# Layer B's gate in the reciprocal's argument at a memory read, and eleven token-row buffers in place of ten

## The chip, the cores and the metric

The kernel runs on one core of a Trainium2 chip. The metric is device time in microseconds (us), as the median of several runs. The kernel before took 1744.88, 1745.94 and 1742.05 us in three runs: median 1744.88 us.

A core has a matrix engine, TensorE (PE; its weight loads are shown apart as PEld), and VectorE (DVE), ScalarE (ACT) and GpSimd (POOL) for the rest. SyncE (SP) does nothing here but issue transfers; ACT and POOL issue some as well. An engine executes its instructions in the order in which they were written to it, so an instruction that waits holds all behind it. Matrix products come to rest in PSUM, of which the kernel uses eight banks of 128 partitions x 512 float32. Everything else lies in SBUF, in buffers that a pool gives out: a new tile takes over the place of an older one, and its first writer waits until the older tile's last reader is done.

## The reference

Four layers A, B, A, B, each added to its input, which is normalised first; 2048 tokens of 640 features, 32 heads of 20 features.

```python
def _A_ref(x, wqkv, wo):                       # linear attention
    phi = lambda t: jnp.where(t > 0, t + 1, jnp.exp(t)) + 1e-6
    pq, pk = phi(q), phi(k)
    kv = jnp.einsum("bhsd,bhse->bhde", pk, v)
    z = jnp.einsum("bhsd->bhd", pk)
    num = jnp.einsum("bhqd,bhde->bhqe", pq, kv)
    den = jnp.einsum("bhqd,bhd->bhq", pq, z)[..., None] + 1e-6
    o = num / den
    return (...)(o, 0, 2, 1, 3).reshape(B, S, D) @ wo

def _B_ref(x, wq, wk, wv, wo, beta):           # attention in 4 segments of 512, with a memory
    g = _sigmoid(beta).reshape(1, H, 1, 1)
    for s in range(N):
        qs, ks, vs = q[:, :, s], k[:, :, s], v[:, :, s]
        p = _softmax(jnp.einsum("bhqd,bhkd->bhqk", qs, ks) * scale + mask, axis=-1)
        a_dot = jnp.einsum("bhqk,bhkd->bhqd", p, vs)
        pq = phi(qs)
        num = jnp.einsum("bhld,bhde->bhle", pq, M)
        den = jnp.einsum("bhld,bhd->bhl", pq, z)[..., None] + 1e-6
        a_mem = num / den
        o = g * a_mem + (1.0 - g) * a_dot
        outs.append(o)
        pk = phi(ks)
        M = M + jnp.einsum("bhld,bhle->bhde", pk, vs)
        z = z + jnp.einsum("bhld->bhd", pk)
    return (...)(jnp.stack(outs, 2)...).reshape(B, S, D) @ wo

x = x + _A_ref(_layernorm(x), A_wqkv, A_wo)
x = x + _B_ref(_layernorm(x), B_wq, B_wk, B_wv, B_wo, B_beta)
...                                            # and both once more
```

The gate g has one value per head: it weighs what is read from the memory against what comes from the segment's own attention.

## The kernel before, in words

**Tiling.** The tokens go in four segments of 512, each of four tiles of 128 tokens (`NT`). A tile of tokens is a *row*: 128 partitions (tokens) x 640 features, 2,560 bytes per partition. For a projection a row is transposed on PE (`turn`, L325), and ACT copies the result from PSUM as fp16 (L329) while DVE writes the remainder, also as fp16 (L330); a projection is then three fp16 products per 128 features, 15 matmuls of 128x320 for half a row (`proj_n`, L401) or 15 of 128x512 for 128 features of a segment (`proj_t`, L387).

**Two streams.** One generator writes the projections and everything that goes with them (`dense`), another the attention of layer B (`attention`): per group of four heads the two fp16 parts of queries and keys are loaded (`stacks`, L994), PE makes scores (L1008) from which DVE takes row maxima (L1015); the maxima are transposed, copied by ACT (L1035) and written into the query stack by two short transfers on SP's queue (L1038); PE makes the scores again with keys on the partitions (L1050), ACT takes exponentials (L1054, tile `pe`), POOL clears what lies over the diagonal (`affine_select`, L1061), PE sums with the values (L1077), ACT evacuates (L1083), and after a transposition the group's 80 features are added to the segment's output `otok` (L1097, L1101). The two streams are woven by modelled costs, and the result is the order on PE, which is kept as written (`MANUAL = ("PE",)`). On the other engines and on the transfer queues a scheduler sets the order: it goes through the program with modelled times, gives each instruction a place when its inputs and its buffer would be free, and so a different number of buffers can give a different order there.

**Row buffers.** Ten buffers of 2,560 bytes per partition are shared by all rows, of whatever kind:

```python
ROWS = 10
return self.sb.tile([P, C, 2, P], F16, tag="row", name="oT", bufs=ROWS)
```

The kinds that occur below: `xo`, the input that is added to a layer's output (loaded, L336); `xn`, a row of that sum; `oT`, a row of attention output, transposed; `x` and `xh`, a loaded row and its normalised form; `pk`, keys of layer A.

**Segment 2's output beside layer 3's first pass.** When the second layer's last segments are still attended to, segment 2's output projection and the first pass of the third layer over segment 0 (`g_first`, with its memory() products, L566) run woven with it, at about 780 to 907 us:

```python
yield from weave(self.g_first(0, x[0], wA, L, over(segs[2])),
                 chain(loads(1), when(segs[2], "attended", out[2]), norms(1)))
```

`out[2]` is `b_out`. Per row it takes an `xo` and an `xn` from the row buffers, starts on the transposition of the next row into another `oT`, and makes the two halves of `xn` in `o_half`: ACT copies a half from PSUM (L478), POOL adds `xo` (L479). The store of `xn` stands on ACT's queue (L977). DVE then gathers the row's moments for the next normalisation, in which `g_norms` takes an `xh` per row, transposes it, and converts it on ACT to fp16 (L514), the remainder on POOL (L515).

```python
x = self.load_x(src, s, i, "xo")
xn = self.row("xn")
t = turned(i + 1) if i + 1 < NT else iter(())
for n in range(2):
    yield from (c for c in [next(t, None)] if c)
    self.o_half(oT[i], wo, "B", x, xn, n, later=not st.get("ends"))
```

**The memory.** `b_project` sums phi(k) v and phi(k) per head as blocks of 128 features (`acc`), with columns of 21 per head: 20 for the numerator, one for the denominator. Blocks off the diagonal are cleared by a product with a pattern, `masked` (L758); the pattern for a read is `gblk` (128x756 float32, 3,024 bytes per partition), which has g in the numerator's columns and 1 in the denominator's. `gates` makes it at the start of the program: g = 1 / (1 + exp(-beta)) by ACT and DVE (L211 is the reciprocal), a copy of the plain pattern `blk` (L214) and five products (L218). `read_mem` reads a memory for one tile of tokens in two halves of 16 heads: matmuls (L456), denominator + 1e-6 (L463), reciprocal (L464), product (L465). Layer A reads its memory by the same function with the plain pattern.

Of the kernel before, what the change touches and what calls it, by code (L numbers as in the profile page):

```python
# [9 lines left out]
F32 = mybir.dt.float32  # L10
F16 = mybir.dt.float16
BF16 = mybir.dt.bfloat16
I32 = mybir.dt.int32
AF = mybir.ActivationFunctionType
OP = mybir.AluOpType
# [5 lines left out]
S, D, H, DH = 2048, 640, 32, 20  # L21
P = 128
C = D // P
SEG = 512
# [3 lines left out]
E1 = DH + 1  # L28
# [6 lines left out]
LO = [(P * t) // DH for t in range(C)]  # L35
HI = [(P * t + P - 1) // DH for t in range(C)]
WID = [(HI[t] - LO[t] + 1) * E1 for t in range(C)]
OFF = [sum(WID[:t]) for t in range(C)]
MW = sum(WID)
VW = H * E1 + 11  # L40
HB = H // 2
# [86 lines left out]
def pause(n):  # L128
    for _ in range(n):
        yield 0.0  # L130
# [12 lines left out]
class Kernel:  # L143
# [14 lines left out]
    def row(self, name):  # L158
        return self.sb.tile([P, D], F32, tag="row", name=name, bufs=ROWS)

# [35 lines left out]
    def gates(self):  # L196


        nc, cp = self.nc, self.cp
        beta = self.A["B_beta"]  # L200
        g = cp.tile([P, H], F32, name="gate")
        nc.sync.dma_start(g, bass.AP(tensor=beta.tensor, offset=beta.offset, ap=[[0, P], [1, H]]))
        self.cg = cp.tile([P, NG], F32, name="cg")
        nc.vector.memset(self.cg, -1e4)
        for h4 in range(4):
            nc.sync.dma_start(self.cg[32 * h4 + DH:32 * h4 + DH + 1],
                              bass.AP(tensor=beta.tensor, offset=beta.offset + h4, ap=[[0, 1], [4, NG]]))
        nc.scalar.activation(g, g, AF.Exp, scale=-1.0)
        nc.scalar.activation(self.cg, self.cg, AF.Exp)
        nc.vector.tensor_scalar(g, g, 1.0, None, op0=OP.add)  # L210
        nc.vector.reciprocal(g, g)  # L211
        nc.vector.tensor_scalar(self.cg, self.cg, 1.0, 2.0 ** 100, op0=OP.add, op1=OP.min)
        self.gblk = cp.tile([P, MW], F32, name="gblk")
        nc.vector.tensor_copy(self.gblk, self.blk)  # L214
        for t in range(C):
            n = HI[t] - LO[t] + 1
            b = self.gblk[:, OFF[t]:OFF[t] + WID[t]].rearrange("p (h e) -> p h e", e=E1)[:, :, :DH]
            nc.vector.tensor_tensor(b, b, g[:, LO[t]:HI[t] + 1, None].to_broadcast([P, n, DH]), op=OP.mult)  # L218

    def w_src(self, key):  # L220
        L, n = key
# [220 lines left out]
        self.vu[k] = user  # L442
        return self.vt[k]

    def read_mem(self, pq, mem, dst):

        nc, sb = self.nc, self.sb
        cut = HB * E1
        for k in range(2):
            nd = self.bank()  # L450
            cost, first = 0, True
            for t in range(C):
                a, b = LO[t] * E1, LO[t] * E1 + WID[t]
                lo, hi = max(a, k * cut), min(b, (k + 1) * cut)
                if lo < hi:
                    nc.tensor.matmul(nd[:, lo - k * cut:hi - k * cut], pq[t],  # L456
                                     mem[:, OFF[t] + lo - a:OFF[t] + hi - a],
                                     start=first, stop=True, skip_group_check=True)
                    first = False
                    cost += 4 * (hi - lo) * COL  # L460
            nd = nd[:, :cut].rearrange("p (h e) -> p h e", e=E1)
            rc = sb.tile([P, HB], F32, tag="rc", name="rc", bufs=3)
            nc.vector.tensor_scalar(rc, nd[:, :, DH], 1e-6, None, op0=OP.add)  # L463
            nc.vector.reciprocal(rc, rc)  # L464
            nc.vector.tensor_tensor(dst[:, k * HN:(k + 1) * HN].rearrange("p (h e) -> p h e", e=DH),  # L465
                                    nd[:, :, :DH], rc[:, :, None].to_broadcast([P, HB, DH]),
                                    op=OP.mult)
            yield cost

    def new_oT(self):  # L470
        return self.sb.tile([P, C, 2, P], F16, tag="row", name="oT", bufs=ROWS)

# [51 lines left out]
    def g_first(self, s, box, w, L, behind=None):  # L524
# [7 lines left out]
        def keys(i):  # L532
            pk.append(sb.tile([P, 2, D + 1], F16, tag="row", name="pk", bufs=ROWS))
            nc.gpsimd.memset(pk[i][:, 0, HN:HN + 1], 1.0)
# [55 lines left out]
    def merge(self, L, wv, wo, memory, fill):  # L590
# [45 lines left out]
        for t in range(C):  # L636
# [3 lines left out]
            for n in range(2):  # L640
                a, b = max(lo, n * HN), min(hi, (n + 1) * HN)
                for c in range(C if a < b else 0):
                    for k, m in ((0, 0), (0, 1), (1, 0)):
# [3 lines left out]
                        first = False  # L647
            k2 = sb.tile([P, 2, SEG], F16, tag="row", name="kt", bufs=ROWS)
            nc.vector.memset(k2, 0.0)
# [217 lines left out]
    def b_project(self, st):  # L867

        nc, sb, bp = self.nc, self.sb, self.bp
        s, w, xT, acc = st["s"], st["w"], st["xT"], st["acc"]  # L870
# [11 lines left out]
        def pk_turn():  # L882
            pt = self.bank()
            for i in range(NT):
                nc.tensor.transpose(pt[:, i * P:(i + 1) * P], pkT[:, i * P:(i + 1) * P], self.ident)
            pk = bp.tile([P, SEG], F32, tag="pkt", name="pkt", bufs=1)
            nc.scalar.activation(pk, pt, AF.Copy)
            return pk
# [13 lines left out]
        for t in range(C):  # L902
            p = yield from self.proj_t(xT, w["q"], t)
            self.split_store(p, st["qd"], t, "q")
            if s > 0:
                pq = sb.tile([P, SEG], F32, tag="pq", name="pq", bufs=PQ)
# [7 lines left out]
            p = yield from self.proj_t(xT, w["k"], t)  # L914
# [10 lines left out]
        def rest():  # L925
            if s == 0:
                yield from pause(4)
            if s < NSEG - 1:
                pk = pk_turn()
                yield 440  # L930
                update(C - 1, pk)
                yield 4 * 4 * WID[C - 1] * COL
                st["mem"] = self.masked(acc, self.gblk)
        st["rest"] = rest()

    def b_memory(self, st, mem):
        st["o"] = self.sb.tile([P, NT, D], F32, tag="big", name="otok", bufs=3)
        if st["s"] > 0:
            for i in range(NT):
                yield from self.read_mem([q[:, i * P:(i + 1) * P] for q in st["pq"]], mem, st["o"][:, i])  # L940
        st["remembered"] = True

    def b_spill(self, st):
# [55 lines left out]
    def row_max(self, G, todo):  # L999

        nc, bp, qs, ks = self.nc, self.bp, G["qs"], G["ks"]
        bs = [self.bank() for _ in range(2)]
        cost = 0
        for p, i, a in todo:
            n = (i + 1) * P
            for par in range(2):
                r = slice(64 * par, 64 * par + 60)
                nc.tensor.matmul(bs[par][:, a:a + n], qs[r, p, i * P:(i + 1) * P], ks[r, p, :n],  # L1008
                                 start=True, stop=True)
                cost += n * COL  # L1010
        for par in range(2):
            for p, i, a in todo:
                n = (i + 1) * P
                junk = bp.tile([P, SEG], BF16, tag="junk", name="junk", bufs=1)
                nc.vector.tensor_tensor_reduce(bs[par][:, a:a + n], bs[par][:, a:a + n], self.maskw[:, SEG - n:],  # L1015
                                               1.0, NEG, OP.add, OP.max, G["mg"][:, par, p, i:i + 1])
        return cost
# [307 lines left out]
                        a.cost = max(a.cost, d.cost)  # L1325


ROWS = 10
PQ = 5
QUEUES = ('gpsimd', 'scalar', 'sync', 'sync', 'gpsimd', 'sync')  # L1330
PE_BUFS = 10
# [33 lines left out]
```

## Time and profile before

| | |
|---|---|
| median of three runs | 1744.88 us |
| the profiled execution | 1743.11 us |
| its span, first to last instruction | 1741.4 us |
| granted clock of TensorE (mean) | 0.998 |
| busy: PE, PEld | 1668.7 us, 1048.4 us |
| busy: DVE, ACT, POOL | 1183.8, 969.3, 518.7 us |
| time on the chain that ended last | PE 77%, DVE 10%, ACT 6% |

PE's time without work is 1741.4 - 1668.7 = 72.7 us. By stretches of the span, worked out from the busy time of each:

| stretch, us | PE idle, us | what runs |
|---|---|---|
| 0 to 100 | 15.0 | start, weights, layer 1 |
| 100 to 200 | 2.7 | layer 1 |
| 200 to 780 | 15.3 | layers 1 and 2 |
| 780 to 840 | 2.0 | attention of layer 2, first pass of layer 3 |
| 840 to 907 | 6.9 | the same, with segment 2's output |
| 907 to 1080 | 0.9 | end of layer 2, layer 3 |
| 1080 to 1741 | 29.5 | layers 3 and 4 |

How lines of the profile are read: a group of instructions stands as line, engine, operation, written tile <- read tiles, partitions x elements, count, then busy time and mean duration in ns of one, then the idle time of the engine before them and what ended most of it. In a timeline a row stands as start, duration, engine, line, operation and tiles, and in square brackets how long the engine had stood idle before and which instruction's end released it. SPq and ACTq are the parts of SP and ACT that issue transfers, and a row that begins "DMA" is a transfer from issue to landing.

### The profile page before, as it was taken

Reading aid. Unit: us, or ns where it says so; the run is one execution under the profiler, and the core shown is the slowest. Engines: PE = TensorE matmul, PEld = TensorE weight load, DVE = VectorE, ACT = ScalarE, POOL = GpSimd, SP = SyncE. Lnnn points to the kernel's source line nnn. Section 1 sums busy time; section 2 is a strip of 40 time slices with the busy share of each in tenths; the row PEclk is TensorE's granted clock in tenths of the full one; section 3 lists DMA queues with packets and bytes.
Section 4 is the critical chain, followed back from the end, with each engine's and each line's share of the span. In section 5 each row is a group of like instructions: output and inputs, shape, how many; then the busy total and the mean of one; then the engine's idle time right before and its main releaser. Section 6 shows DMA issues by size and latency. Waiting matters only on the chain.

```text
span 1741.4 us, 36031 instructions
## 1 busy us (share of the span) xinstructions
PE 1668.7 (96%) x13032; PEld 1048.4 (60%) x13032; DVE 1183.8 (68%) x3856; ACT 969.3 (56%) x1818; POOL 518.7 (30%) x982
## 2 busy tenths in 40 slices
PE   6999999999999999999989999999999999999998
PEld 4676666654665566456556777666546545645555
DVE  8645534577787677758864466846778877878773
ACT  5545433357557646667665553333675576666674
POOL 1543350022123312333342311220422432333452
PEclk9999999999999999999999999999999999999999
DMA  7422453422322322352211303433232323223432
GB/s 264 181 109 95 155 188 105 136 70 81 118 69 70 113 93 81 124 191 67 78 43 39 114 31 122 159 105 124 66 105 83 112 80 106 102 81 111 137 108 92
DMA packets 118330, 187.59 MB, mean 108 GB/s; under 512 B 13948, under 2 KB 79612, under 8 KB 115848
## 3 DMA queue, kind: packets, MB, share of 16 engines
q1 hardware_dynamic: 105896, 142.68, 25.7%
q0 software_dynamic: 3040, 21.63, 3.4%
q10 hardware_dynamic: 9216, 20.98, 3.1%
q8 instruction: 103, 1.69, 0.4%
q14 instruction: 75, 0.61, 0.1%
HBM read 106.05 MB, written 78.64 MB: 106 GB/s over the span
## 4 chain that ended last, share of the span: by engine, by line
PE 77%; DVE 10%; ACT 6%; issue 2%; POOL 2%; DMA 2%; SPq 0%; ACTq 0%; POOLq 0%; DVEq 0%
PE ps L401 32%; PE ps L387 17%; PE ps L1077 8%; PE ps L1050 4%; PE ps L1008 3%; ACT pe L1054 3%; PE ps L325 3%; PE ps L566 3%; PE ps L456 3%; DVE ps L1015 2%; PE ps L1090 1%; PE ps L893 1%; PE ps L732 1%; DVE st L344 1%; DVE oT L330 1%
## 5 line engine op out<-in xcount | busy, mean ns | idle before, releaser
L1015 DVE CUSTOM_DVE_ANT_0 ps<-ps,maskw 128x512 f32<-128x512 f32 (+3 forms) x1024 | 472.8, 520 | 40.4 <-PE ps L1008 38.1
L1054 ACT ACTIVATE pe<-ps,lsc 128x512 f32<-128x512 f32 x640 | 395.0, 696 | 91.1 <-PE ps L1050 88.0
L1061 POOL TENSOR_SCALAR_AFFINE_SELECT pe<-pe 128x256 f32<-128x256 f32 (+1 forms) x640 | 230.1, 365 | 448.8 <-ACT pe L1054 434.9
L401 PEld LDWEIGHTS <-xT 128*128 128x128 f16 x2880 | 280.6, 98 | 114.8 <-issue 10.2
L401 PEld LDWEIGHTS <-oT 128*128 128x128 f16 x1920 | 186.1, 98 | 80.3 <-issue 6.5
L1077 PE MATMUL ps<-pe,v 128*32 128x512 f32 (+3 forms) x2048 | 161.4, 436 | 13.3 <-POOL pe L1061 6.9
L401 PE MATMUL ps<-w_Bo,oT 128*128 128x320 f16 x960 | 142.4, 301 | 2.5 <-ACT pe L1054 1.0
L1015 DVE DVE_READ_ACCUMULATOR2_ANT mg<- 128x1 f32 x1024 | 144.7, 141 | 0.0
L387 PE MATMUL ps<-xT,w_Bq 128*128 128x512 f16 x600 | 140.2, 379 | 1.9 <-ACT pe L1054 0.8
L401 PE MATMUL ps<-w_Bv,xT 128*128 128x320 f16 x960 | 139.7, 299 | 0.7 <-DVE otok L1097 0.6
L387 PE MATMUL ps<-xT,w_Bk 128*128 128x512 f16 x600 | 138.8, 379 | 1.2 <-ACT pe L1054 1.2
L401 PE MATMUL ps<-w_Ak,xT 128*128 128x320 f16 x960 | 136.1, 299 | 0.5 <-ACT r L415 0.5
L1008 PE MATMUL ps<-ks,qs 60*128 60x512 f16 (+3 forms) x1024 | 124.6, 297 | 8.9 <-ACT pe L1054 3.2
L858 DVE SCALAR_TENSOR_TENSOR nat<-ps,nat 128x512 f16<-128x512 f32 x80 | 55.2, 690 | 87.9 <-ACT nat L857 87.8
L1077 PEld LDWEIGHTS ps<-pe,v 128*32 128x32 f32 x2048 | 64.9, 109 | 73.4 <-issue 44.9
L1050 PE MATMUL ps<-qs,ks 62*128 62x512 f16 (+3 forms) x1024 | 105.7, 300 | 3.1 <-ACT pe L1054 1.1
L427 POOL TENSOR_SCALAR e<-e 128x320 f32<-128x320 f32 (+1 forms) x52 | 82.9, 1595 | 82.1 <-ACT e L423 77.9
L857 ACT ACTIVATE nat<-ps 128x512 f16<-128x512 f32 x80 | 48.2, 603 | 90.9 <-PE ps L387 71.6
L387 PEld LDWEIGHTS <-w_Bk 128*128 128x128 f16 x600 | 57.3, 98 | 65.4 <-issue 5.6
L387 PEld LDWEIGHTS <-w_Bq 128*128 128x128 f16 x600 | 56.7, 98 | 65.8 <-issue 7.8
L1008 PEld LDWEIGHTS <-qs 60*128 60x128 f16 x1024 | 50.3, 94 | 75.0 <-issue 47.7
L349 POOL TENSOR_TENSOR rs<-rs,mhalf 128x1 f32<-128x1 f32 x48 | 27.6, 576 | 218.7 <-DVE rs L348 218.7
(220 smaller groups left out, 2633.1 us busy)
## 6 DMA issues: line engine op xcount, KB each, us to landing
x<-xn ACTq DMA_DIRECT2D x48, 320.0 KB
qs<-qd SPq DMA_DIRECT2D x128, 120.0 KB
ks<-kd SPq DMA_DIRECT2D x128, 120.0 KB
xo<-x SPq DMA_DIRECT2D x48, 320.0 KB
pqi<-pqd SPq DMA_DIRECT2D x32, 320.0 KB
qd<-nat SPq DMA_DIRECT2D x40, 256.0 KB
kd<-nat SPq DMA_DIRECT2D x40, 256.0 KB
x<-in_A_x SPq DMA_DIRECT2D x16, 320.0 KB
```

What stands on the lines that cost most here:

```text
L325: nc.tensor.transpose(pt[:, (c - c0) * P:(c - c0 + 1) * P], src[:, c * P:(c + 1) * P], self.ident)
L387: nc.tensor.matmul(p, w[:, c, a, t * P:(t + 1) * P], xT[:, c, b, :], start=k == 0, stop=k == 3 * C - 1)
L401: nc.tensor.matmul(p, xT[:, c, a, i * P:(i + 1) * P], w[:, c, b, n * HN:(n + 1) * HN], start=k == 0, stop=k == 3 * C - 1)
L427: nc.gpsimd.tensor_scalar(e, e, 1.0, eps, op0=OP.min, op1=OP.add)
L456: nc.tensor.matmul(nd[:, lo - k * cut:hi - k * cut], pq[t], mem[:, OFF[t] + lo - a:OFF[t] + hi - a], start=first, stop=True, skip_group_ch ...
L858: nc.vector.scalar_tensor_tensor(nat[:, 1], p, QK_SHIFT, nat[:, 0], op0=OP.mult, op1=OP.subtract)
L1008: nc.tensor.matmul(bs[par][:, a:a + n], qs[r, p, i * P:(i + 1) * P], ks[r, p, :n], start=True, stop=True)
L1015: nc.vector.tensor_tensor_reduce(bs[par][:, a:a + n], bs[par][:, a:a + n], self.maskw[:, SEG - n:], 1.0, NEG, OP.add, OP.max, G["mg"][:, p ...
L1050: nc.tensor.matmul(b[:, a:a + n], ks[r, p, j * P:(j + 1) * P], qs[r, p, j * P:], start=True, stop=True)
L1054: nc.scalar.activation(e, b, AF.Exp, scale=self.lsc)
L1061: nc.gpsimd.affine_select(d, d, pattern=pat, compare_op=OP.is_ge, fill=0.0, base=0, channel_multiplier=-1)
L1077: nc.tensor.matmul(G["pv"][32 * h4:32 * h4 + 32, j * P:], v[j][:, h * E1:h * E1 + 32], G.pop((p, par, j)), start=j == 0, stop=j == 2, skip ...
```

## The change

`gates` stops at 1 + exp(-beta), which `self.ginv` keeps; the reciprocal, the tile `gblk`, its copy and its five products are gone. A layer B memory is now masked with the plain pattern. In `read_mem`, layer B passes `ginv`, and the argument of the reciprocal is made in one instruction with two tensor operands, (denominator + 1e-6) * (1 + exp(-beta)); its reciprocal is g / (denominator + 1e-6). Layer A passes nothing and keeps its form. In `row_max` a tile `junk` (128x512 bf16, 1,024 bytes per partition), which nothing reads or writes, is no longer asked for. The rows go from ten buffers to eleven.

```diff
@@ gates
         nc.vector.tensor_scalar(g, g, 1.0, None, op0=OP.add)
-        nc.vector.reciprocal(g, g)
         nc.vector.tensor_scalar(self.cg, self.cg, 1.0, 2.0 ** 100, op0=OP.add, op1=OP.min)
-        self.gblk = cp.tile([P, MW], F32, name="gblk")
-        nc.vector.tensor_copy(self.gblk, self.blk)
-        for t in range(C):
-            n = HI[t] - LO[t] + 1
-            b = self.gblk[:, OFF[t]:OFF[t] + WID[t]].rearrange("p (h e) -> p h e", e=E1)[:, :, :DH]
-            nc.vector.tensor_tensor(b, b, g[:, LO[t]:HI[t] + 1, None].to_broadcast([P, n, DH]), op=OP.mult)
+        self.ginv = g
@@ read_mem
-    def read_mem(self, pq, mem, dst):
+    def read_mem(self, pq, mem, dst, ginv=None):
...
-            nc.vector.tensor_scalar(rc, nd[:, :, DH], 1e-6, None, op0=OP.add)
+            if ginv is None:
+                nc.vector.tensor_scalar(rc, nd[:, :, DH], 1e-6, None, op0=OP.add)
+            else:
+                nc.vector.scalar_tensor_tensor(rc, nd[:, :, DH], 1e-6, ginv[:, k * HB:(k + 1) * HB],
+                                               op0=OP.add, op1=OP.mult)
             nc.vector.reciprocal(rc, rc)
@@ b_project, rest()
-                st["mem"] = self.masked(acc, self.gblk)
+                st["mem"] = self.masked(acc, self.blk)
@@ b_memory
-                yield from self.read_mem([q[:, i * P:(i + 1) * P] for q in st["pq"]], mem, st["o"][:, i])
+                yield from self.read_mem([q[:, i * P:(i + 1) * P] for q in st["pq"]], mem, st["o"][:, i],
+                                         self.ginv)
@@ row_max
-                junk = bp.tile([P, SEG], BF16, tag="junk", name="junk", bufs=1)
@@
-ROWS = 10
+ROWS = 11
```

PE's order is the same in both programs. On DVE, ACT, POOL and SP rows move in the stretch described above, where segment 2's output runs beside layer 3's first pass. The line numbers of the changed program are smaller by up to eight: its L476, L477 and L976 are L478, L479 and L977 of before, its L323 is L329, L330 is L336, L361 is L367, L1033, L1036, L1052, L1059, L1081 and L1099 are L1035, L1038, L1054, L1061, L1083 and L1101.

ACT before, at the row of segment 2's output whose `xn` is written first in the stretch. `pe` are exponentials, `oT` copies the next transposed row (3 and then 2 of its 5 blocks), `mt` the maxima, `oTf` the evacuated sums, `xn` the two halves of the output row, and DMA its store:

```order
L1054 ACTIVATE pe<-ps,lsc 128x512 x4
L329 ACTIVATE oT<-ps 128x3x128
L329 ACTIVATE oT<-ps 128x2x128
L1054 ACTIVATE pe<-ps,lsc 128x512 x2
L1035 ACTIVATE mt<-pm 32x128
L1083 ACTIVATE oTf<-ps,cg 128x512
L1054 ACTIVATE pe<-ps,lsc 128x512 x4
L478 ACTIVATE xn<-ps,ioB 128x320 x2
L1054 ACTIVATE pe<-ps,lsc 128x512
L977 DMA x_88<-xn 128x640
L1054 ACTIVATE pe<-ps,lsc 128x512 x4
L478 ACTIVATE xn<-ps,ioB 128x320 x2
```

The same place after:

```order
L323 ACTIVATE oT<-ps 128x2x128
L407 ACTIVATE e<-ps,inv_Aq 128x320
L409 ACTIVATE r<-ps,inv_Aq 128x320
L1052 ACTIVATE pe<-ps,lsc 128x512 x4
L476 ACTIVATE xn<-ps,ioB 128x320 x2
L1052 ACTIVATE pe<-ps,lsc 128x512 x2
L976 DMA x_88<-xn 128x640
L1033 ACTIVATE mt<-pm 32x128
L1081 ACTIVATE oTf<-ps,cg 128x512
L476 ACTIVATE xn<-ps,ioB 128x320
L1052 ACTIVATE pe<-ps,lsc 128x512 x4
L476 ACTIVATE xn<-ps,ioB 128x320
```

The copies of `oT` have moved ahead of the exponentials of the group before and of layer 3's queries (L407, L409); both halves of the first `xn` and its store stand one batch of exponentials earlier; and the halves of the second `xn` come one at a time, on either side of the next four exponentials.

POOL before, at the same place. `pe` are the selects on the exponentials, `xn` the additions of `xo`, `otok` the addition of a group of heads, `rs` the power in the moments of a segment:

```order
L1101 TENSOR_TENSOR otok<-otok,tmp 128x4x80
L1061 AFFINE_SELECT pe<-pe 128x128 x4
L479 TENSOR_TENSOR xn<-xn,xo 128x320 x2
L1061 AFFINE_SELECT pe<-pe 128x2x128 x5
L479 TENSOR_TENSOR xn<-xn,xo 128x320 x2
L1061 AFFINE_SELECT pe<-pe 128x2x128
L367 TENSOR_TENSOR rs_12196<-rs_12196,mhalf 128x4
```

POOL after:

```order
L1059 AFFINE_SELECT pe<-pe 128x2x128 x4
L477 TENSOR_TENSOR xn<-xn,xo 128x320 x2
L1059 AFFINE_SELECT pe<-pe 128x2x128 x2
L477 TENSOR_TENSOR xn<-xn,xo 128x320
L1099 TENSOR_TENSOR otok<-otok,tmp 128x4x80
L1059 AFFINE_SELECT pe<-pe 128x128 x4
L477 TENSOR_TENSOR xn<-xn,xo 128x320
L1059 AFFINE_SELECT pe<-pe 128x2x128 x4
L361 TENSOR_TENSOR rs_11684<-rs_11684,mhalf 128x4
```

The first `xn`'s additions have moved ahead of the last two wide selects of the group before and of the four narrow ones after them; the second `xn`'s stand around those four.

SP before, in the same stretch. `qs<-mt` writes maxima into a query stack, `qs<-qd` and `ks<-kd` load the stacks, `pqd` stores layer 3's queries:

```order
L552 DMA pqd_0_10215<-e 128x320 x2
L1038 DMA qs<-mt 2x8x128 x2
L994 DMA qs<-qd 60x2x512 x2
L994 DMA ks_2759<-kd 60x2x512 x2
L336 DMA xo<-x_87 128x640
L1038 DMA qs<-mt 2x8x128 x4
```

SP after:

```order
L550 DMA pqd_0_9823<-e 128x320 x2
L330 DMA xo<-x_87 128x640
L1036 DMA qs<-mt 2x8x128 x2
L993 DMA qs<-qd 60x2x512 x2
L993 DMA ks_2751<-kd 60x2x512 x2
L1036 DMA qs<-mt 2x8x128 x4
```

The load of `xo` has moved ahead of two writes of maxima and of the loads of a group's stacks.

## The prediction

> **What bounds the kernel now.** I read the page's busy shares and chain first, then the busy time by stretches, to find where TensorE (PE) is not working, then the timelines of the engines in the one stretch where the row buffers are waited for.
>
> ```profile
> PE 1668.7 (96%) x13032; PEld 1048.4 (60%) x13032; DVE 1183.8 (68%) x3856; ACT 969.3 (56%) x1818; POOL 518.7 (30%) x982
> ...
> PE 77%; DVE 10%; ACT 6%; issue 2%; POOL 2%; DMA 2%; SPq 0%; ACTq 0%; POOLq 0%; DVEq 0%
> ```
>
> PE bounds the kernel: it is busy for 1668.7 of 1741.4 us. The order on PE is written out by the kernel and the change leaves it alone, so time can come only out of the 72.7 us in which PE stands idle, and go only into new idle time. So: which of those idle places does a row buffer make?
>
> ```profile
> 40.00:60.00 20.00, 18.23 (x133) 12.99 (x131) 15.84 (x36) 14.46 (x29) 10.10 (x7) 1.00 0.37 130
> 60.00:80.00 20.00, 20.00 (x111) 11.98 (x110) 12.28 (x37) 8.46 (x12) 11.83 (x11) 1.00 0.72 251
> ...
> 780.00:840.00 60.00, 57.98 (x525) 36.99 (x518) 53.58 (x198) 43.63 (x89) 24.23 (x51) 1.00 0.29 94
> 840.00:907.00 67.00, 60.13 (x514) 35.20 (x512) 47.51 (x172) 40.72 (x77) 25.34 (x52) 1.00 0.19 58
> 907.00:1080.00 173.00, 172.12 (x1314) 123.49 (x1313) 91.39 (x210) 95.34 (x195) 34.53 (x67) 1.00 0.21 70
> ```
>
> Columns: stretch, length, busy time of PE, PEld, DVE, ACT, POOL. From 780 to 840 us PE idles 60.00 - 57.98 = 2.02 us, 3.4%. From 840 to 907 us, where the same attention runs beside segment 2's output and the third layer's first pass, it idles 67.00 - 60.13 = 6.87 us, 10%, though DVE, ACT and POOL are all less busy per us there. From 907 to 1080 us it idles 0.88 us in 173. Whatever is won before 907 us is therefore carried on: what follows is PE's own work in a fixed order.
>
> ```profile
> 856.27 0.55 PE L325 MATMUL ps<-ident,otok 128*128 128x128 f32 x3
> ...
> 863.63 2.21 PE L401 MATMUL ps<-w_Bo,oT 128*128 128x320 f16 x15
> ...
> 874.13 2.20 PE L401 MATMUL ps<-w_Bo,oT 128*128 128x320 f16 x15 [0.20 <-ACT pe L1054]
> ...
> 877.50 0.63 PE L1008 MATMUL ps<-ks,qs 60*128 60x384 f16 x4 [0.63 <-DVE oT L330]
> ...
> 900.12 0.63 PE L1077 MATMUL ps<-pe,v 128*32 128x256 f32 x6 [1.81 <-POOL pe L1061]
> ```
>
> ```profile
> 876.37 0.76 ACT L329 ACTIVATE oT<-ps 128x384 f16<-128x384 f32 x2 [1.13 <-PE ps L401]
> ...
> 890.62 0.94 ACT L478 ACTIVATE xn<-ps,ioB 128x320 f32<-128x320 f32 x2 [2.77 <-PE ps L401]
> ...
> 892.94 0.36 ACTq L977 DMA_DIRECT2D x<-xn  x1
> 893.34 2.46 ACT L1054 ACTIVATE pe<-ps,lsc 128x512 f32<-128x512 f32 x4 [1.20 <-POOL pe L1061]
> 897.43 0.94 ACT L478 ACTIVATE xn<-ps,ioB 128x320 f32<-128x320 f32 x2 [1.63 <-DMA x<-xn]
> ```
>
> Read these together. The three transposes of 856.27 wait in a PSUM bank until 876.37, when ACT copies them out; what ends that copy's wait is not the transpose but the projection that ended at 876.33 (874.13 + 2.20), the last reader of the older oT whose row the new oT takes. The two projections of 863.63 and 874.13 fill one xn; ACT takes both halves at 890.62, when the next projection has read its oT. That is 16 to 25 us of bank time for results that were finished. The next xn (897.43) waits for a store of an earlier xn, and everything queued behind it on ACT and POOL waits too: PE then stands 1.81 us. So in this stretch the wait that ends last is often for one of ten row buffers, and PE feels it as a full bank or a late exponential.
>
> **The change part by part.**
>
> *Start.* Seven DVE instructions go.
>
> ```profile
> L211 DVE RECIPROCAL gate<-gate x1: 333/333/333, 41.2 to 41.2; 128x32 f32<-128x32 f32 x1
> ...
> L214 DVE CAST gblk<-blk x1: 545/545/545, 74.6 to 74.6; 128x756 f32<-128x756 bf16 x1
> ...
> L218 DVE TENSOR_TENSOR gblk<-gblk,gate x5: 296/298/319, 75.7 to 76.6; 128x140 f32<-128x140 f32 x4, 128x160 f32<-128x160 f32 x1
> ```
>
> They cost 0.33 + 0.55 + 5 x 0.30 = 2.4 us of DVE. At 74.6 to 76.9 us PE is busy for all of its slice (20.00 of 20.00): nothing gained. At 41.2 us PE's slice has idle time, so that one is worth 0 to 0.33 us; I take 0, since PE's work of that slice waits on weights and not on the gate.
>
> *Masks.* Six products of a memory read the plain pattern in place of the gated one.
>
> ```profile
> L758 DVE TENSOR_TENSOR mem<-acc,gblk x6: 932/946/948, 347.9 to 1490.2; 128x756 f32<-128x756 f32 x6
> L758 DVE TENSOR_TENSOR mem<-acc,blk x1: 945/945/945, 242.8 to 242.8; 128x756 f32<-128x756 f32 x1
> ```
>
> The plain pattern already stands in one row: 945 against 946 ns. Cost 0.
>
> *Gate at the read.* Layer B's memory reads, 48 by the first row below, take a scalar_tensor_tensor with a second tensor operand where a tensor_scalar stood.
>
> ```profile
> L465 DVE TENSOR_TENSOR otok<-ps,rc 128x320 f32<-128x320 f32 x48 | 23.2, 488 | 0.6
> ...
> L481 DVE SCALAR_TENSOR_TENSOR xn<-ps,ioG,xo 128x320 f32<-128x320 f32 x32 | 17.1, 546 | 4.0 <-PE ps L401 3.9
> ...
> L1025 DVE SCALAR_TENSOR_TENSOR m<-mg,m 128x16 f16<-128x16 f32 x64 | 12.8, 200 | 1.4
> ...
> L463 DVE TENSOR_SCALAR rc<-ps 128x16 f32<-128x16 f32 x80 | 12.3, 158 | 7.1 <-PE ps L456 7.0
> ```
>
> No such instruction of 128x16 from PSUM is shown. From above: 546 - 488 = 58 ns, what a longer form of the new kind takes over a product of the same size; from below 0, as the longer reading can hide behind the instruction before. The nearest row by size is L1025, 200 - 158 = 42 ns. 48 x 42 ns = 2.0 us of DVE (bounds 0 and 2.8 us). DVE is ended upon by PE only rarely (it is 10% of the chain), and of these reads 0.1 us is what I put on the path, with 2.0 us as the end for the range. The Trainium skill, Perfetto Trace Analysis, under "Optimizing Scalar/DVE Operations", has the fixed cost of a DVE instruction depend on engine and memory, some 60 ns on SBUF and 125 ns on PSUM, so both forms would cost the same and this term would be nothing, the sum 0.1 us better. The rows above do not bear it out: the PSUM form at 158 ns is shorter than the SBUF form at 200 ns.
>
> *Eleventh row.* This is the term that counts. If the stretch 840 to 907 us idled like the one before it, 3.4% of some 62 us is 2.1 us, and 6.87 - 2.1 = 4.8 us would go. Order and rows of the changed program support it: the copy of oT moves ahead of both query pairs, the first xn's first half ahead of a query pair, and the next xn stands right after the projections that fill it. Three things give some back.
>
> ```profile
> 877.78 0.41 POOL L1061 TENSOR_SCALAR_AFFINE_SELECT pe<-pe 128x256 f32<-128x256 f32 x1 [2.07 <-ACT pe L1054]
> 878.35 0.41 POOL L1061 TENSOR_SCALAR_AFFINE_SELECT pe<-pe 128x256 f32<-128x256 f32 x1 [0.17 <-ACT pe L1054]
> ...
> 891.23 1.68 POOL L479 TENSOR_TENSOR xn<-xn,xo 128x320 f32<-128x320 f32 x2 [3.02 <-ACT xn L478]
> ```
>
> (i) POOL now adds both halves of xn (1.68 us) ahead of these two selects. ACT can evacuate from 876.3, so POOL adds from 876.9 to 878.6 and the selects end near 879.5 instead of 878.8. PE needs them in the last of the matmuls over weights that run from 878.07 for some 2.3 us, near 879.9: 0.4 us of cover. I take 0; without the cover it is 0.7 us.
>
> ```profile
> 892.94 4.41 DMA x<-xn
> ```
>
> (ii) The xn after it takes the row of the xn before in the changed program too, so ACT again waits for a store to land, 4.41 us after its issue. Issued at 878.7 it lands near 883.1; the half it makes room for is projected by 884.6, less the 1 to 2 us won by then. I take 0.3 us (bounds 0 and the 1.63 us that this wait takes now). (iii) Four conversions to fp16 (L514) stand ahead of the next four exponentials where two stood: at most 2 x 0.7 = 1.4 us of ACT; I take 0.4, as ACT's waits of 1.20 and 1.63 us above it are then gone.
>
> On SyncE one load of xo moves ahead of two row loads and four stack loads (L1038, L994). It waits for POOL's second add, 878.6 us.
>
> ```profile
> 879.60 1.29 SPq L1038 DMA_DIRECT2D qs<-mt  x2
> ```
>
> The row loads behind it start at 879.60 for their own reason, so 1 us covers the load; beyond that every us late is a us for the maxima that PE's scores need.
>
> Elsewhere the eleventh row lets loads of xo, x and pqi start earlier, but in those stretches PE is full or waits for something else: 0, bounds 0 and 0.5 us of gain.
>
> *Sum.* -4.8 + 0.3 + 0.4 + 0.1 = -4.0 us. The profiled execution took 1743.11 us (span 1741.4 and 1.7 around it), 1.8 under the median of 1744.88; so 1739.1 for it and 1740.9 us for the median, 0.23% faster. About 0.2%, 3.5 us, is what a measurement of this kernel tells from no change.
>
> **The rivals.**
>
> *The wait only moves.* The row is there, but store and adds in (i) to (iii) cost what they can, 0.7 + 1.6 + 1.4 = 3.7 us, and DVE's term up to 1: 4.8 - 4.7 leaves 0.1 us, 1744.8. For it: two of the four waits named are again before the four exponentials. Against: the banks are emptied 14 us sooner in any case, and 0.63 + 1.81 us of PE's idle time hang on that alone.
>
> *Slower: the store holds ACT.* ACT's evacuation of the second xn stands ahead of four exponentials and waits for the store. If the store lands d us after PE has the half ready, ACT, POOL's adds, SyncE's load and the maxima behind it are all d late. At 4.41 us d is near 0; the gain is eaten at d = 4.0, a landing 8.4 us after issue, and 0.2% is lost at d = 7.5, 11.9 us. A transfer as long stands in the trace, though of a wide weight load among others:
>
> ```profile
> 144.36 9.41 DMA stage<-in_B_wk
> ```
>
> Together with DVE's 2.0 us that gives 1744.9 + 9.41 - 4.41 - 4.0 + 2.0, about 1748. Against: the DMA engines are busy for 0.19 of the stretch only.
>
> *More than the idle time.* The Trainium skill, Perfetto Trace Analysis, "Identifying the Most-Contended Engine", calls matmul busy time a poor measure and weight-load busy time a good one. As a mechanism here: PEld is busy for 36.99 of 60.00 us and then for 35.20 of 67.00; at the first rate the second stretch takes 35.20 x 60.00 / 36.99 = 57.1 us, 9.9 us less: 1735.0. Against:
>
> ```profile
> 882.53 2.04 PE ps L401 x15
> ...
> 940.94 6.11 PE ps L401 x45
> ```
>
> Fifteen projection matmuls take 2.04 us in the stretch as in the full one after it (6.11 / 3), so PE does not work slower there; the mix differs.
>
> **How the numbers follow.** Row waits go, gain 2.7 to 5.5 us: 0.63, of which 0.48 is over 3.5 us. The wait moves, within 2.7 us of before: 0.20. Slower by over 0.2%: 0.12. More than the idle time: 0.05. So faster 0.53, same 0.15 + 0.20 = 0.35, slower 0.12. The likeliest is 1740.9, its own range 1738.0 (all of the 6.87 us) to 1742.5. The range for 8 in 10 runs from 1737.0, that end less 1 us of scatter, to 1746.5, no gain and most of DVE's 2.0 us.
>
> **What would show it.** Right: ACT's oT copy follows its transposes by a few us and not 20; both halves of the first xn leave PSUM within 1 us of their projections; PE's idle time from 840 to about 903 us is near 2.5 us; the work after it starts 4 us earlier and keeps that; the 48 reads take near 200 ns. Wrong: PE's idle time there stays above 5 us, with ACT xn waiting for the store, or POOL's adds, as what ends it; or the stretches with memory reads (480 to 520, 640 to 680, 780 us and their like in the fourth layer) grow by more than 0.5 us each.

## The result, and the profile after

The changed kernel takes 1738.34 us in the median of seven runs (1736.07 to 1741.17) against 1744.88 us: ratio 0.9963, 95% interval 0.9954 to 0.9973, so 6.5 us less (4.7 to 8.0). Forecast were 1740.9 us. Its profiled execution took 1736.07 us, with a span 7.0 us shorter than before.

From the page after, the engines' busy shares and the shares of the chain that ended last:

```profile
PE 1666.1 (96%) x13032; PEld 1047.5 (60%) x13032; DVE 1180.9 (68%) x3849; ACT 969.7 (56%) x1818; POOL 517.7 (30%) x982
...
PE 78%; DVE 10%; ACT 6%; issue 2%; POOL 2%; DMA 1%; SPq 1%; ACTq 0%; POOLq 0%; DVEq 0%
```

PE's order is the same in both, so every matmul of one profile has its partner in the other, and a stretch can be cut at the same two matmuls. Two stretches hold nearly all that changed. Busy time by stretches, before:

```profile
840.07:920.05 79.98, 72.86 (x629) 43.09 (x627) 55.59 (x200) 49.27 (x93) 32.25 (x65) 1.00 0.16 49
640.08:780.12 140.04, 135.00 (x1105) 79.59 (x1107) 100.03 (x366) 86.55 (x159) 45.14 (x103) 1.00 0.36 116
```

The same matmuls after:

```profile
841.13:912.88 71.75, 70.26 (x629) 42.71 (x627) 54.50 (x200) 49.33 (x93) 32.01 (x65) 1.00 0.18 55
639.87:781.19 141.32, 135.36 (x1105) 79.58 (x1108) 100.11 (x366) 86.64 (x159) 45.14 (x103) 1.00 0.36 117
```

The stretch with segment 2's output is 8.23 us shorter. Of these, 5.63 us are PE's idle time (79.98 - 72.86 = 7.12 before, 1.49 after); the other 2.60 us came out of PE's busy time. From 640 to 780 us 1.28 us were lost. All the rest of the span nets to less than 0.1 us.

What PE waited for in the first stretch, after (us in all, times, longest): the whole list, where before had twelve such entries and 1.8 us for POOL's selects alone.

```profile
PE ps L1075 <- DVE oT L324: 0.7, 1, 0.7
PE ps L395 <- ACT r L409: 0.3, 1, 0.3
PE ps L1007 <- DVE mg L1013: 0.2, 1, 0.2
```

The timeline of PE after, and behind it that of ACT:

```profile
857.10 0.55 PE L319 MATMUL ps<-ident,otok 128*128 128x128 f32 x3
...
864.18 2.21 PE L395 MATMUL ps<-w_Bo,oT 128*128 128x320 f16 x15
...
873.21 2.20 PE L395 MATMUL ps<-w_Bo,oT 128*128 128x320 f16 x15 [0.27 <-ACT r L409]
```

```profile
860.18 0.49 ACT L323 ACTIVATE oT<-ps 128x384 f16<-128x384 f32 x1
...
875.45 0.94 ACT L476 ACTIVATE xn<-ps,ioB 128x320 f32<-128x320 f32 x2
...
877.79 0.35 ACTq L976 DMA_DIRECT2D x<-xn  x1
...
883.31 0.53 ACT L476 ACTIVATE xn<-ps,ioB 128x320 f32<-128x320 f32 x1 [3.34 <-PE ps L395]
```

The three transposes end at 857.65 and are copied 2.5 us later, not 20. Both halves of the first xn leave PSUM when the second projection ends (875.41) and not 14 us behind it. The second xn, whose row comes free when the store issued at 877.79 has landed, is held up by its own projection and not by the store: what ends ACT's wait of 3.34 us is PE.

The reads of the memory on DVE after, gated (L460) and plain (L458); before, the same 48 took 152 ns and the same 32 took 167 ns in the mean, which together are the 158 ns of the group in the prediction:

```profile
L460 DVE SCALAR_TENSOR_TENSOR rc<-ps,gate 128x16 f32<-128x16 f32 x48 | 7.1, 151 | 0.1
L458 DVE TENSOR_SCALAR rc<-ps 128x16 f32<-128x16 f32 x32 | 5.3, 166 | 7.0 <-PE ps L450 6.9
```

### The profile page after: what moved, and what is told of

The parts are those of the page before. It is cut to its first block, busy times and chain, and to the rows that moved or that the text cites. A ratio compares the mean times of both kernels' runs of the same rounds, so it can differ in the third digit from the quotient of the medians.

```text
span 1734.4 us, 36014 instructions
## 1 busy us (share of the span) xinstructions
PE 1666.1 (96%) x13032; PEld 1047.5 (60%) x13032; DVE 1180.9 (68%) x3849; ACT 969.7 (56%) x1818; POOL 517.7 (30%) x982
## 4 chain that ended last, share of the span: by engine, by line
PE 78%; DVE 10%; ACT 6%; issue 2%; POOL 2%; DMA 1%; SPq 1%; ACTq 0%; POOLq 0%; DVEq 0%
PE ps L395 32%; PE ps L381 17%; PE ps L1075 7%; PE ps L1048 4%; ACT pe L1052 3%; PE ps L1007 3%; PE ps L319 3%; PE ps L564 3%; PE ps L450 3%; DVE ps L1013 2%; PE ps L1088 1%; PE ps L891 1%; PE ps L730 1%; DVE st L338 1%; DVE xn L479 1%
## 5 line engine op out<-in xcount | busy, mean ns | idle before, releaser
L1052 ACT ACTIVATE pe<-ps,lsc 128x512 f32<-128x512 f32 x640 | 394.8, 696 | 87.6 <-PE ps L1048 84.9
L1059 POOL TENSOR_SCALAR_AFFINE_SELECT pe<-pe 128x256 f32<-128x256 f32 (+1 forms) x640 | 229.7, 365 | 449.2 <-ACT pe L1052 444.0
```

What stands on the lines that cost most here:

```text
L1052: nc.scalar.activation(e, b, AF.Exp, scale=self.lsc)
L1059: nc.gpsimd.affine_select(d, d, pattern=pat, compare_op=OP.is_ge, fill=0.0, base=0, channel_multiplier=-1)
```

## The experiments

The theory, ROW: all of the gain is waits for a row buffer between 840 and 907 us. Its rivals: GATE, that the smaller DVE work gives a part; and ANY, that room or the number of rows counts wherever it is given. In the table, "627 matmuls" is the length of the stretch that begins at 840 us of before, "waits" PE's idle times of 0.1 us and more in it, and "640 to 780" the length of the other stretch, all worked out from the starts of PE's matmuls in the one profiled execution.

| kernel | median, us | ratio to before | 627 matmuls, us | waits | 640 to 780, us |
|---|---|---|---|---|---|
| before | 1744.88 | | 79.99 | 17 | 140.04 |
| after | 1738.34 | 0.9963 (0.9954 to 0.9973) | 71.76 | 5 | 141.31 |
| gate_ten_rows | 1744.37 | 1.0001 (0.9992 to 1.0010) | 79.51 | 18 | 139.94 |
| row_with_gblk | 1740.36 | 0.9975 (0.9966 to 0.9985) | 71.75 | 5 | 141.09 |
| row_gblk_same_ring | 1738.55 | 0.9970 (0.9959 to 0.9980) | 71.76 | 5 | 140.78 |
| own_oT3 | 1736.84 | 0.9956 (0.9944 to 0.9969) | 72.61 | 7 | 139.74 |
| own_xn2 | 1740.79 | 0.9981 (0.9972 to 0.9990) | 75.04 | 12 | 140.40 |
| own_xn3 | 1745.27 | 1.0005 (0.9997 to 1.0014) | 79.28 | 12 | 139.78 |
| rows_twelve | 1737.76 | 0.9960 (0.9946 to 0.9974) | 72.97 | 7 | 141.04 |
| exps_eleven | 1744.45 | 0.9998 (0.9989 to 1.0007) | 79.90 | 17 | 139.94 |
| after_again | 1738.57 | 0.9965 (0.9952 to 0.9979) | 72.29 | 5 | 141.41 |
| after_third | 1736.02 | 0.9957 (0.9944 to 0.9970) | 71.80 | 5 | 141.25 |
| own_oT3_again | 1737.60 | 0.9960 (0.9946 to 0.9973) | 72.63 | 7 | 140.47 |
| pairs_apart | 1736.30 | 0.9958 (0.9943 to 0.9972) | 71.88 | 5 | 141.00 |

**Gate or row.** The gate edit alone:

```diff
 (the changed kernel)
-ROWS = 11
+ROWS = 10
```

> The changed kernel with ten rows: the gate in the reciprocal's argument and no junk tile, but no eleventh buffer. PE, ACT, POOL and SP then have the order of before. Theory ROW (all of the gain is waits for a row buffer between 840 and 907 us): no gain, 1744.9 us within 1.5, PE idle 6 to 7.5 us from 840 to 907. Rival GATE (the part of the gain above the forecast 4.0 us, 2.5 us, comes from the 3 us of DVE work that are gone): 1742.4 us or less.

No gain, and the stretch stands as it was:

```profile
840.74:920.25 79.51, 72.86 (x630) 43.06 (x628) 55.45 (x200) 49.30 (x93) 32.28 (x65) 1.00 0.15 49
```

The row alone, in two forms that differ in where its room comes from:

```diff
 (the kernel before)
-        self.gblk = cp.tile([P, MW], F32, name="gblk")
+        self.gblk = cp.tile([P, MW], F16, name="gblk")
-                junk = bp.tile([P, SEG], BF16, tag="junk", name="junk", bufs=1)
-ROWS = 10
+ROWS = 11
 # row_with_gblk
-        g = cp.tile([P, H], F32, name="gate")
+        g = self.sb.tile([P, 512], F32, tag="er", name="gate", bufs=3)[:, :H]
 # row_gblk_same_ring
-        self.ones = cp.tile([1, P], F32, name="ones")
+        self.ones = self.g_last[:1, :P]
```

> The kernel before with eleven rows: the gated pattern stays, in float16 to make room, and the reads keep the tensor_scalar. ACT, POOL and SP then have the order of the changed kernel. ROW: the whole gain, 1738.3 us within 1.5, and the 627 matmuls that begin at 840 us of before take about 71.8 us. GATE: 1740.9 us or more.

> As row_with_gblk, but the room comes from the row of ones, and the gate keeps its own tile. In row_with_gblk the gate lay in one of the three buffers tagged er, and PE waited 1.88 us for the first memory read at 245 us, which no other kernel shows. If the shifted turn of that ring is the cause, this wait is gone and the kernel as fast as after: 1738.5 us within 1. GATE: 1740.4 us again, the 1.9 us being the gate's.

In both the stretch is as short as after, to 0.01 us. The first form missed 1.8 us of the gain (1740.36 against 1738.57 us of after_again on the same chip), so that neither theory's time came, and its trace shows where: PE's first memory read of layer A came late (first row: PE; below it ACT, in whose ring of three `er` buffers the gate had shifted the turns, so that its relu waits for DVE's use of a buffer; in the second form no relu there waits for DVE, and PE does not wait).

```profile
245.66 0.93 PE L456 MATMUL ps<-mem,pqi 128*128 128x147 f32 x6 [1.88 <-issue]
```

```profile
237.56 0.69 ACT L425 ACTIVATE r<-ps,inv_Aq 128x512 f32<-128x512 f32 x1 [0.92 <-DVE pk L428]
...
240.06 0.69 ACT L425 ACTIVATE r<-ps,inv_Aq 128x512 f32<-128x512 f32 x1 [1.24 <-DVE pq L428]
```

With the ring left alone the row brings the whole gain, 1738.55 us. GATE is out on both sides: with ten rows and with eleven, the gate at the read makes no difference that these runs can tell.

**Which tile.** Ten rows, the gate at the read, and one buffer of its own for a single tile in segment 2's output of layer 2 (rows counted from 0: oT3 and xn3 belong to its last row):

```diff
 # own_oT3; own_xn2 and own_xn3 do the same for xn with i == 2, i == 3
+        if own:
+            return self.sb.tile([P, C, 2, P], F16, tag="own", name="oT", bufs=1)
...
-            oT.append(self.new_oT())
+            oT.append(self.new_oT(norm and s == 2 and i == 3))
```

> Ten rows and the gate at the read, and one buffer of its own for a single tile: the fourth oT of segment 2's output in layer 2. In before this tile takes the place of the third oT, and the third xn takes the place of this one. ROW: these two places are the cause, so most of the gain comes back with this one tile: 1738.5 us within 2, ACT's copy of it within 5 us of its transposes. Rival ANY (it is the number of rows over the whole program that counts): a quarter of the gain or less, 1743 us or more.

> Ten rows, the gate at the read, and the buffer of its own now for the third xn of segment 2's output (in before it takes the place of the fourth oT, and leaves PSUM at 890.62 us). The fourth oT still takes the third one's place. ROW, by the gaps of PE in before: the waits up to 880 us stay (2.3 of the 8.2 us by which the stretch is longer), those behind them go, some 6 us: 1739 us within 1.5, ACT's oT copy still 15 to 20 us behind its transposes, xn evacuated within 3 us of its projections. ANY: 1743 us or more.

> The same with the fourth xn alone in the buffer of its own: in before it is the one that waits for a store to land (1.63 us of ACT, then 1.81 us of PE). ROW: only that wait goes, 2 to 2.6 us: 1742.4 us within 1.3; the third xn still leaves PSUM 14 us late. If the store's wait were the cause of the whole, 1738.5 us.

own_oT3 brings all of the gain. ACT's rows there, the copy of oT3 and both halves of the third xn:

```profile
859.12 0.52 ACT L323 ACTIVATE oT<-ps 128x384 f16<-128x384 f32 x1
...
874.47 0.94 ACT L478 ACTIVATE xn<-ps,ioB 128x320 f32<-128x320 f32 x2
```

own_xn2 frees only the xn. The oT copy stays as late as before, and 5.0 of the 8.2 us go, where 6 were expected; the median, 3.5 us under before's of the same chip, lies 0.3 us above the expected span:

```profile
869.05 0.53 ACT L476 ACTIVATE xn<-ps,ioB 128x320 f32<-128x320 f32 x1 [1.67 <-PE ps L395]
...
878.64 0.76 ACT L323 ACTIVATE oT<-ps 128x384 f16<-128x384 f32 x2 [0.55 <-PE ps L395]
```

own_xn3 brings nothing, against the 2 to 2.6 us expected. The wait for the store is gone; in its place POOL, with the half in hand, waits for the load of that row's `xo`, and the selects behind it on POOL are late by as much (POOL, then PE):

```profile
895.63 1.67 POOL L477 TENSOR_TENSOR xn<-xn,xo 128x320 f32<-128x320 f32 x2 [2.43 <-DMA xo<-x]
897.26 1.49 POOL L1062 TENSOR_SCALAR_AFFINE_SELECT pe<-pe 128x256 f32<-128x256 f32 x4
```

```profile
897.72 1.84 PE L1078 MATMUL ps<-pe,v 128*32 128x384 f32 x20 [1.66 <-POOL pe L1062]
```

`xo` takes the row of the `xo` before it, which POOL reads only once the late third xn is out. So the store, the last wait of the chain in the profile, was not its cause: the two places that oT3 and the third xn shared were. A buffer given just anywhere does not do it.

**More rows, or other room.** In rows_twelve the room for a twelfth row comes from the plain pattern in one byte an element; in exps_eleven the eleventh buffer goes to the exponentials.

```diff
 # rows_twelve (the changed kernel)
-        self.blk = cp.tile([P, MW], BF16, name="blk")
+        self.blk = cp.tile([P, MW], mybir.dt.uint8, name="blk")
-        self.ones = cp.tile([1, P], F32, name="ones")
+        self.ones = self.g_last[:1, :P]
-ROWS = 11
+ROWS = 12
 # exps_eleven (the changed kernel)
-ROWS = 11
-PE_BUFS = 10
+ROWS = 10
+PE_BUFS = 11
```

> The changed kernel with twelve rows (room from the plain pattern kept in one byte an element and from a row of ones that lies in a tile used only later). ROW: in the stretch only 1.5 us of idle time are left, of which rows end none; so 0 to 1 us less than with eleven, 1737.5 to 1738.5 us. ANY: another gain like the first, 1734 us or less. If eleven rows cost 1.2 us between 640 and 780 us because the rows change places there, twelve change them again and the 141.3 us of that stretch may go either way by 1.2.

> Ten rows and the gate at the read, the room given to an eleventh buffer of exponentials (2,048 bytes) in place of a row. The orders are those of before. ROW: exponentials wait for no buffer in the stretch, so nothing is gained: 1744.5 us within 1.5, PE idle 6 to 7.5 us from 840 to 907 us. ANY room: 1741 us or less.

Neither gains on its base. Twelve rows leave the time where eleven put it (the stretch is 1.2 us longer than with eleven), and room given to the exponentials is worth nothing: ANY is out.

**Twice the same.** The changed kernel again, and own_oT3 again beside it.

> The changed kernel once more, for what differs between two executions of one program. The wait of PE before the scores at 708 us was 1.54 us in the profile after against 1.00 before, and the stretch from 640 to 780 us as a whole 1.3 us longer. If this is scatter of transfers, another execution shows 1.0 to 1.6 us at 708 and a stretch that differs by 0.5 us or more; if it is the gate at the reads, it shows 1.54 and 1.3 again. Median 1738.3 within 1 us.

> The kernel with one own buffer for the fourth oT again, beside the changed kernel on one chip. If ten shared rows spare the 1.2 us that eleven or twelve cost from 640 to 780 us (139.8 to 140.4 us in the four ten-row profiles taken since, 140.8 to 141.4 in the five with more), it is again 1 to 1.7 us under the changed kernel: 1737 us. If that was scatter, both are equal within 0.7 us.

> The changed kernel beside it: 1738.4 us within 1, and 141 to 141.4 us from 640 to 780 us of before.

The changed kernel's stretch came out again, 72.29 and 71.80 us. Two forecasts here were missed: after_third is 2.4 us faster than expected, and own_oT3_again, which was to be equal to after_third or under it, is 1.6 us over it.

The stretch from 640 to 780 us takes 139.74 to 140.47 us in the seven profiles with ten rows and 140.78 to 141.41 us in the seven with eleven or twelve. The two groups do not overlap, and it is not the gate (row_with_gblk and row_gblk_same_ring have none at the reads): more shared rows go with about 1.1 us in a stretch where no instruction has another place in the order of its engine. Between matmuls of PE, in the means of the two groups, 0.7 us of it lie at 663 us of before, 0.25 us at the maxima's landing at 707 us and 0.2 us at 736 us. At the first of these DVE makes an xn whose `xo` has only just been loaded; here in after_third, DVE and then PE:

```profile
662.43 0.55 DVE L479 SCALAR_TENSOR_TENSOR xn<-ps,ioA,xo 128x320 f32<-128x320 f32 x1 [1.04 <-DMA xo<-in_A_x]
```

```profile
664.02 0.77 PE L319 MATMUL ps<-ident,xh 128*128 128x128 f32 x5 [0.61 <-DVE xn L479]
```

In gate_ten_rows, own_oT3 and own_xn3 neither waits there. In the other four profiles with ten rows both do, for 0.4 to 0.6 us, so part of the difference at this place is scatter: own_oT3_again is the program of own_oT3. Before, DVE and then PE:

```profile
662.00 0.55 DVE L481 SCALAR_TENSOR_TENSOR xn<-ps,ioA,xo 128x320 f32<-128x320 f32 x1 [0.44 <-DMA xo<-in_A_x]
```

```profile
663.59 0.77 PE L325 MATMUL ps<-ident,xh 128*128 128x128 f32 x5 [0.54 <-DVE xn L481]
```

With another number of buffers a row takes over from another row. But SP issues this load at the same time in all fourteen profiles, to 0.1 us, counted from the same matmul at 640 us. DVE starts on it 4.1 to 4.8 us behind the issue with ten rows and 4.9 to 5.4 us with more. So the issue is not what is late; why the load lands later stays open. own_oT3 saves the 1.1 us and loses 0.8 us in the first stretch, so it is not the better version: 1736.84 and 1737.60 against 1738.57 and 1736.02 us on the same chips.

**Where the busy time went.** The last experiment asked why PE's busy time fell with the same matmuls.

```diff
 (the changed kernel, row_max)
-        for p, i, a in todo:
-            n = (i + 1) * P
-            for par in range(2):
+        for par in range(2):
+            for p, i, a in todo:
+                n = (i + 1) * P
```

> The changed kernel with another order of PE's matmuls in row_max: of a list with two entries a and b, both matmuls on partitions 0 to 59 first and then both on 64 to 123 (a0 b0 a1 b1), where a0 a1 b0 b1 stood. The work is the same. It tests why PE's busy time fell by 2.6 us in the stretch though the matmuls are the same. Theory SIDE BY SIDE (two matmuls on different partitions run at the same time, and a wait between them costs that overlap besides its idle time): three lists in a group have two entries, two of 384 and 128 columns and one of 256 and 256; by 0.435 ns a column (382 less 215 ns over 384 columns in the profile after) each loses the overlap of its first entry's pair, 2 x 167 + 111 = 445 ns, and 64 groups lose 28 us of PE: 1755 to 1768 us. Rival RECORDS (the busy time is only drawn differently when there is a wait): 1738.5 us within 2.

The time did not grow: 1736.30 us, as after_third on the same chip (1736.02), so by its letter the expectation of SIDE BY SIDE failed, and RECORDS' time was missed by 0.2 us. But the trace shows that a premise of SIDE BY SIDE failed, that PE runs such matmuls in the order written: the second matmul of 384 columns starts at 877.51 us, and the first of 128, which the program has ahead of it, at 877.66. Six score matmuls, pairs_apart and then after:

```profile
877.28 0.60 PE L1007 MATMUL ps<-ks,qs 60*128 60x512 f16 x6
```

```profile
875.57 0.60 PE L1007 MATMUL ps<-ks,qs 60*128 60x512 f16 x6
```

They have 512, 384 and 128 columns, two of each. The profile's groups of after, by form, give 512 columns and 128 columns apart:

```profile
L1007 PE MATMUL ps<-ks,qs 60*128 60x512 f16 x256 | 50.9, 382 | 0.7 <-DVE mg L1013 0.3 <-ACT pe L1052 0.2
...
L1007 PE MATMUL ps<-ks,qs 60*128 60x128 f16 x256 | 31.0, 215 | 0.0
```

So a column takes (382 - 215) / 384 = 0.435 ns, and 215 - 128 x 0.435 = 159 ns are left that do not grow with the columns. One after the other the six would take 2048 x 0.435 = 891 ns and the 159; two at a time 1024 x 0.435 = 445 and 159, the 0.60 us of both rows. They run side by side in either order, so the experiment did not take the overlap away and can't price it. The arithmetic prices something else: while PE flows, those 159 ns lie under the next matmul; where PE waits, the last matmul ahead of the wait can show them, as busy time in which nothing new begins. Four matmuls of 256 columns that did not wait take 0.39 us in the first row, of after; in the rows below it, of before, with a wait among them, 0.27 + 0.38 = 0.65 us:

```profile
872.56 0.39 PE L1007 MATMUL ps<-ks,qs 60*128 60x256 f16 x4
```

```profile
872.98 0.27 PE L1008 MATMUL ps<-ks,qs 60*128 60x256 f16 x1 [0.49 <-ACT r L415]
873.55 0.38 PE L1008 MATMUL ps<-ks,qs 60*128 60x256 f16 x3 [0.31 <-ACT pe L1054]
```

From start to start of the same matmuls, 2.57 of the 2.60 us stand at the matmul just ahead of one of before's 17 waits, so it is the waits that the busy time went with. Shared among the twelve fewer it is 2.60 / 12 = 0.22 us each: 0.16 us are this fixed part; that the rest is pairs which started apart is argued from rows like the last two, not shown by a run.

And 0.22 us is a mean, not a price. With two waits more than after, own_oT3 is busy in the stretch for 70.27 us, against 70.26; with seven more, own_xn2 is busy for 70.85 us and own_xn3 for 73.13 us. The number of waits alone does not give the busy time. RECORDS is not ruled out either: the profile models the ends of matmuls, and with them the border between busy and idle. The 8.23 us lie between two starts and do not hang on it.

## Why the prediction was right, and where it was off

*What bounds it and where.* Right: PE's order did not move, the gain lies where the prediction put it, and what followed kept it (the matmuls from 920 to 1080 us all start 7.17 us earlier). The chain it read, oT waiting for the older oT and xn for the next projection, is what own_oT3 and own_xn2 take apart. One reading was off: the banks were held for 14 us (876.33 to 890.62) to 25 us, not from 16.

*Eleventh row, -4.8 us.* The sign and the mechanism were right, the size was not, and this is the term that was off. It took from PE's idle time what was over the 3.4% of the stretch before. The idle time fell by 5.63 us, to 2.1%; and the stretch lost 2.60 us of busy time besides, which the sum had no term for: it took the idle time for all that a wait costs. Three prices that it set against the gain, 0.8 us together, were not paid. So 4.0 + 0.83 + 2.60 + 0.80 = 8.23 us, twice the sum. That the median still lies in the range given as its own, 0.3 us from the end that stood for all of the idle time, is luck: the loss elsewhere hides part of what the stretch gave.

*(i) POOL's additions ahead of two selects, 0.* Right: the list of PE's waits after has none for POOL. *(ii) The store, 0.3.* Not paid; the projection ends later than the landing. own_xn3 shows that even before, taking this wait away uncovers another of the same length. *(iii) Conversions ahead of exponentials, 0.4.* Not paid: the one wait near them is 0.18 us, for DVE.

*Gate at the read, 0.1 us.* 151 ns against 152 for the form that was there at the same 48 reads: 0, the lower bound. The row chosen as nearest, 128x16 at 200 ns, misled. The Trainium skill, Perfetto Trace Analysis, "Optimizing Scalar/DVE Operations", has the overhead of a DVE instruction depend on engine and memory. The trace agrees in that both forms cost the same here; the prediction set it aside wrongly. *Start and masks, 0.* Right, by gate_ten_rows.

*Elsewhere, 0 to 0.5 us of gain.* Wrong: 1.28 us of loss from 640 to 780 us between these two profiles, about 1.1 us in the means above, from a cause that stays open. This and the 8.23 us make the 7.0 us between the profiles.

*The rivals.* "The wait only moves" is false for the eleventh row and true for own_xn3. "Slower" did not come about: the store had landed. "More than the idle time" was given 0.05, since fifteen projection matmuls take 2.04 us in both stretches. That row stays true, and yet the matmuls of 840 to 907 us took 8.39 us less, 1.5 us more than their idle time of 6.87: matmuls are not slower there, but busy time went with the waits. So this rival came true in the stretch, though not for the kernel. The Trainium skill, Perfetto Trace Analysis, "Identifying the Most-Contended Engine", does not hold matmul busy time to be a good measure; the trace agrees, as the same 627 matmuls were busy for 72.86 us before and 70.26 us after. The 9.9 us worked out by weight loads were 1.5 us too many for the stretch.

*What would show it.* PE's idle time from 840 to 907 us is 1.46 us on the same matmuls (forecast near 2.5), the work behind starts 7.17 us earlier (4), and the 48 reads take 151 ns (200). The halves of the first xn were to leave PSUM within 1 us of their projections. The second does (0.04 us); the first, projected by 866.39, leaves 9.1 us later, with the second. It cost PE no wait: none of the three in the list is for ACT's xn. Of the signs of being wrong, growth by more than 0.5 us where memories are read: 640 to 680 us grew by 0.43 us here, and by 0.53 in row_with_gblk, which has no gate at its reads.

## What to carry to other kernels

Where tiles of several kinds share a ring of buffers, ask for each waiting writer whose place it takes and when that place's last reader runs: one buffer for the one tile with the bad neighbour was worth as much here as one more for all, and a buffer for the tile that showed the last wait was worth nothing. A wait of a pipelined engine can cost more than its idle time: a third of what was gained in the stretch stood as busy time, so compare the same work from start to start and not the idle time alone. A change in a ring's size or turn changes neighbours everywhere: a small tile put into a ring of three cost 1.8 us here, and an eleventh row went with 1.1 us lost in a stretch that it was not made for.

## What the runs showed of the hardware

Matmuls that read other partitions (0 to 59 and 64 to 123) run side by side even where the program has them apart: in pairs_apart the second matmul of 384 columns starts 0.01 us behind the first and 0.15 us ahead of one of 128 columns that the program has between them, so the order written is not strictly the order of the starts. The Trainium skill, TensorEngine Tiling (Array Packing), "Key Properties", says that tiles operate independently; the 0.60 us for 2048 columns, 0.435 ns each, agree.

PE's granted clock falls for some 3 us at a few places, and not in every execution. Stretches of 4 us, after and then before:

```profile
1638.00:1642.00 4.00, 3.96 (x20) 2.29 (x22) 1.10 (x3) 1.15 (x3) 0.81 (x2) 0.62 0.29 117
```

```profile
1684.00:1688.00 4.00, 4.00 (x23) 2.23 (x22) 1.96 (x9) 1.76 (x4) 1.22 (x3) 0.62 0.02 6
```

Fifteen projection matmuls take 3.65 us in the first, where 2.20 is usual, so such a place lengthens PE's work by about 1.5 us. It need not lengthen the program: after_again lacks the fall that after has near 1093 us, and the 1.58 us that its matmuls save there are waited out right behind them (worked out from the starts of the same matmuls). Before's fall at 1684 us came although no wait of PE in the 7 us ahead of it was longer than 0.86 us.
